# Pairing heads in a cached-decode attention kernel: one softmax chain, accumulator and eviction for two heads, and two value buffers instead of three

## The chip, the core and the metric

The kernel runs on one core of one Trainium2 chip. The core has five engines that follow instruction streams of their own: TensorE (PE, with its weight loads as PEld), VectorE (DVE), ScalarE (ACT), GpSimd (POOL) and SyncE (SP); SP issues nearly all loads here, and sixteen DMA engines carry them out. TensorE writes to PSUM, all else lies in SBUF. The metric is the device time of one execution in microseconds (us). The times of the kernel before are 528.05, 528.24 and 528.86 us, median 528.24.

## What is computed

One decode step for four sequences: a layer norm, attention over the last 2048 positions of a cache with 32 heads of width 192, and a gated feed-forward block beside it; the residual is added at the end. All inputs and the output are bf16.

```python
def _A_ref(x, k_cache, v_cache, wq, wo):
    B, Sq, D = x.shape                       # 4, 1, 640
    Hq, Dh = 32, 192
    Hkv, Sk = k_cache.shape[1], k_cache.shape[2]   # 32, 8192
    W = min(4096, max(256, Sk // 4))         # 2048
    q = (x @ wq).reshape(B, Sq, Hq, Dh).transpose(0, 2, 1, 3)
    k = k_cache[:, :, Sk - W:, :]
    v = v_cache[:, :, Sk - W:, :]
    scores = jnp.einsum("bhqd,bhkd->bhqk", q, k) * (Dh ** -0.5)
    p = _softmax(scores, axis=-1)
    o = jnp.einsum("bhqk,bhkd->bhqd", p, v)
    return o.transpose(0, 2, 1, 3).reshape(B, Sq, Hq * Dh) @ wo

def _B_ref(x, w1, w3, w2):                   # 640 -> 1536 -> 640
    return (silu(x @ w1) * (x @ w3)) @ w2

xn = _layernorm(x, axis=-1)
out = x + _A_ref(xn, A_k_cache, A_v_cache, A_wq, A_wo) + _B_ref(xn, B_w1, B_w3, B_w2)
```

## The kernel before

**Layout.** For each head, keys and values of all four sequences are one tile of 128 partitions: a partition holds 64 consecutive positions of one sequence (NJ = 64), 192 numbers each, 24 KB. So a key or value load is 3,072 KB, and there are 32 of each. wq (7.5 MB) is loaded at the start into the three value buffers, wo in eight loads of 960 KB, one for four heads; w1, w3 and w2 use key buffers at the end.

**Scores on VectorE.** Each query is broadcast to 128 partitions once per two heads (`q_bcast`, L207). A head is worked in four chunks of 16 positions (CH = 16, NC = 4). `mult` (L216) multiplies keys and query elementwise into a bf16 product tile `pr` of 16 x 192. `adder` (L225) adds slices of the product on TensorE: six matmuls (192/32) with the identity accumulate 16 x 32 sums in PSUM. `reduce_tile` (L233) finishes the sum over 32 on VectorE and writes 16 scores.

**Softmax chain.** After the last chunk of a head: the row maximum (`chain_lmax`, L243), its transpose on TensorE (`chain_tr`, L248), the maximum per sequence (`chain_gmax`, L253), its way back to all partitions by a matmul and the bias of each sequence (`chain_bc`, L261), four exponentials on ScalarE, one for each sequence, into a zero-padded tile `z`, each with its row sum. `rowsum` (L274) turns the row sums into a reciprocal.

**Values on TensorE.** `pv` (L281) runs 32 matmuls per head with `z` as weights and the values as moving data, 8 in each slot, into one PSUM accumulator; ScalarE evicts it to `o_sb`. `fold` (L297) adds the partial rows, and scales them. `ge_tr` (L308) and `ge_proj` (L315) transpose four heads' outputs and multiply them by their part of wo, into an accumulator held in PSUM over the whole kernel.

**Order.** The calls are put into slots, one for each chunk (128 in all), and phases within a slot; the calls are then made slot by slot. L363 to L404 hold the table: a load of keys eight slots ahead of the head's first product, a load of values nine slots after it less eight, `pv` nine slots after the chunk's product. This is the order in which the program is written; a scheduler in the compiler then sorts each engine's instructions by when it expects their inputs, with earlier calls first. An edge fixes one more thing: the reduction of chunk s comes after the product of chunk s + RLAG (L240, RLAG = 2). SP issues loads in its order, and an issue waits until the buffer that it will fill is free; whatever is behind it on SP waits too.

**Buffers.** Three for keys, three for values, four for products, three for `z`, two for wo.

**The end.** From slot 124 on w1, the last values, w3, the last part of wo and w2 are queued behind each other; the feed-forward matmuls run between the last heads' steps, and the last 160 KB of w2 release the last eight matmuls, an addition and two stores.

Of the kernel before, what the change touches and what calls it, by code (L numbers as in the profile page):

```python
# [18 lines left out]
def kernel(  # L19
# [12 lines left out]
    DD: int = 32,  # L32
    CH: int = 16,
    HG: int = 4,
    QP: int = 2,
    KBUFS: int = 3,
    VBUFS: int = 3,
    PBUFS: int = 4,
    NZ: int = 3,
    L: int = 9,  # L40
    RLAG: int = 2,
    ALIGN: int = 128,
):

    nc = tc.nc
# [14 lines left out]
    RPP = (HG * Dh) // P  # L62
    QW = QP * Dh
    OW = HG * Dh
# [4 lines left out]
    assert (HG * Dh) % P == 0 and Dh % RPP == 0 and H % HG == 0 and HG % QP == 0  # L69
# [10 lines left out]
    wpool = ctx.enter_context(tc.tile_pool(name="wstream", bufs=2))  # L80
    ppool = ctx.enter_context(tc.tile_pool(name="pr", bufs=PBUFS))
    qpool = ctx.enter_context(tc.tile_pool(name="qbc", bufs=2))
# [15 lines left out]
    def load_k(h):  # L98
        kt = kpool.tile([P, NJ, Dh], BF16, tag="kt")
        nc.sync.dma_start(out=kt[:], in_=cache_rows(A_k_cache, h))  # L100
        kts[h] = kt

    def load_v(h):
        vt = vpool.tile([P, NJ, Dh], BF16, tag="vt")
        nc.sync.dma_start(out=vt[:], in_=cache_rows(A_v_cache, h))
        vts[h] = vt

    def wo_load(hg):
        wt = wpool.tile([P, RPP * D], BF16, tag="w")
        nc.sync.dma_start(out=wt[:], in_=A_wo[hg * OW:(hg + 1) * OW, :].rearrange("(p i) n -> p (i n)", i=RPP))  # L110
        wos[hg] = wt

    x_sb = const.tile([B, D], BF16, name="x_sb")
# [12 lines left out]
    for r0 in range(0, KC, RV):  # L126
        r1 = min(r0 + RV, KC)
        wt = vpool.tile([P, RV, H * Dh], BF16, tag="vt")
        nc.sync.dma_start(out=wt[:, 0:r1 - r0, :], in_=wq_rows[:, r0:r1, :])  # L129
        wqs.append(wt)  # L130
# [9 lines left out]
    nsc = const.tile([1, B], FP32, name="nsc")  # L140
    nc.vector.memset(nsc[:], -SCALE)

    zs = []
    for i in range(NZ):
        z = const.tile([P, NJ // 2, 32], BF16, name=f"z{i}")
        nc.gpsimd.memset(z[:], 0.0)
        zs.append(z)
    oTs = []
    for i in range(2):
        oT = const.tile([P, RPP, 32], BF16, name=f"oT{i}")  # L150
        nc.gpsimd.memset(oT[:], 0.0)
        oTs.append(oT)
    rowsel = const.tile([P, 2 * B], FP32, name="rowsel")
    nc.vector.tensor_reduce(out=rowsel[:], in_=idf[:].rearrange("p (g c) -> p c g", g=NG)[:, 0:2 * B, :], axis=AX.X, op=ALU.add)
# [9 lines left out]
    sq = ppool.tile([B, D], FP32, tag="pr")  # L164
    ssq = const.tile([B, 1], FP32, name="ssq")
    nc.scalar.activation(out=sq[:], in_=xc[:], func=ACTF.Square, accum_out=ssq[:])
# [6 lines left out]
    xn = const.tile([B, D], BF16, name="xn")  # L173
# [13 lines left out]
    mbias = const.tile([P, B], FP32, name="mbias")  # L187
    nc.vector.tensor_scalar(out=mbias[:], in0=selT[:], scalar1=-1.0, scalar2=-MASK, op0=ALU.add, op1=ALU.mult)
# [27 lines left out]
    def mult(s):  # L216
        h, c = s // NC, s % NC
        pr = ppool.tile([P, CH, Dh], BF16, tag="pr")
        mi = nc.vector.tensor_tensor(out=pr[:], in0=kts[h][:, c * CH:(c + 1) * CH, :],  # L219
                                     in1=qbcs[h // QP][:, h % QP, :].unsqueeze(1).to_broadcast([P, CH, Dh]),  # L220
                                     op=ALU.mult)
        prs[s] = pr
        mult_insts[s] = mi

# [8 lines left out]
    def reduce_tile(s):  # L233
        h, c = s // NC, s % NC
        if c == 0:
            sc = small.tile([P, NJ], FP32, tag="sc", bufs=3)
            scs[h] = sc
        ri = nc.vector.tensor_reduce(out=scs[h][:, c * CH:(c + 1) * CH], in_=pss.pop(s)[:], axis=AX.X, op=ALU.add)  # L238
# [4 lines left out]
    def chain_lmax(h):  # L243
        lmax = small.tile([P, 1], FP32, tag="lmax")
        nc.vector.tensor_reduce(out=lmax[:], in_=scs[h][:], axis=AX.X, op=ALU.max)  # L245
        chs[h] = [lmax]

    def chain_tr(h):  # L248
        mt = ps_t.tile([P, P + B], FP32, tag="t")
        nc.tensor.transpose(out=mt[0:1, 0:P], in_=chs[h][0][:], identity=idf[:])  # L250
        chs[h].append(mt)

    def chain_gmax(h):  # L253
        gmax = small.tile([1, B], FP32, tag="gmax")
        nc.vector.tensor_reduce(out=gmax[:], in_=chs[h][1][0:1, 0:P].rearrange("o (q b) -> o b q", b=B),
                                axis=AX.X, op=ALU.max)
        gmq = small.tile([1, NQ, B], FP32, tag="gmq", bufs=1)
        nc.vector.tensor_copy(out=gmq[:], in_=gmax[:].unsqueeze(1).to_broadcast([1, NQ, B]))  # L258
        chs[h].append(gmq)

    def chain_bc(h):  # L261
        lmax, mt, gmq = chs.pop(h)
        sc = scs.pop(h)
        nc.tensor.matmul(mt[:, P:P + B], lhsT=gmq[:].rearrange("o q b -> o (q b)"), rhs=nsc[:], start=True, stop=True)  # L264
        negm = small.tile([P, B], FP32, tag="negm")
        nc.vector.tensor_tensor(out=negm[:], in0=mt[:, P:P + B], in1=mbias[:], op=ALU.add)  # L266
        z = zs[h % NZ][:].rearrange("p j (s b) -> p j s b", b=B)
        rs = small.tile([P, B], FP32, tag="rs")
        for b in range(B):
            nc.scalar.activation(out=z[:, :, 0:2, b], in_=sc[:].rearrange("p (j s) -> p j s", s=2), func=ACTF.Exp,  # L270
                                 bias=negm[:, b:b + 1], scale=SCALE, accum_out=rs[:, b:b + 1])
        rss[h] = rs

    def rowsum(h):  # L274
        tb = ps_t.tile([B, 1], FP32, tag="t")
        nc.tensor.matmul(tb[:], lhsT=rss.pop(h)[:], rhs=ones_f[:], start=True, stop=True)  # L276
        rcp = small.tile([B, 1], FP32, tag="rcp")
        nc.vector.reciprocal(out=rcp[:], in_=tb[:])  # L278
        rcps[h] = rcp

    def pv(s):  # L281
        h, c = s // NC, s % NC
        if c == 0:
            o_ps = ps_o.tile([P, 2 * Dh], FP32, tag="o_ps")
            o_pss[h] = o_ps
        o_ps, z, vt = o_pss[h], zs[h % NZ], vts[h]
        for jj in range(c * CH // 2, (c + 1) * CH // 2):
            g = jj % NG
            nc.tensor.matmul(o_ps[32 * g:32 * g + 32, :], lhsT=z[:, jj, :], rhs=vt[:, 2 * jj:2 * jj + 2, :],  # L289
                             start=(jj < NG), stop=(jj >= NJ // 2 - NG))  # L290
        if c == NC - 1:
            o_sb = opool.tile([P, 2, Dh], FP32, tag="o_sb")
            nc.scalar.copy(out=o_sb[:].rearrange("r two d -> r (two d)"), in_=o_pss.pop(h)[:])  # L293
            o_sbs[h] = o_sb
            vts.pop(h)

    def fold(h):  # L297
        hg, hl = h // HG, h % HG
        fp = ps_t.tile([B, Dh], FP32, tag="t")
        o_sb = o_sbs.pop(h)  # L300
        for two in range(2):
            nc.tensor.matmul(fp[:], lhsT=rowsel[:, two * B:(two + 1) * B], rhs=o_sb[:, two, :], start=(two == 0), stop=(two == 1))  # L302
        if hl == 0:
            o_bf = opool.tile([B, HG, Dh], BF16, tag="o_bf")
            o_bfs[hg] = o_bf
        nc.vector.tensor_scalar_mul(out=o_bfs[hg][:, hl, :], in0=fp[:], scalar1=rcps.pop(h)[:, 0:1])  # L306

    def ge_tr(hg):  # L308
        gp = ps_t.tile([P, RPP, B], BF16, tag="t")
        of = o_bfs.pop(hg)[:].rearrange("r h d -> r (h d)")  # L310
        for i in range(RPP):
            nc.tensor.transpose(out=gp[:, i, :], in_=of[:, i:OW:RPP], identity=idb[0:B, 0:B])  # L312
        nc.vector.tensor_copy(out=oTs[hg % 2][:, :, 0:B], in_=gp[:])  # L313

    def ge_proj(hg, i):  # L315
        oT = oTs[hg % 2]
        wo_t = wos[hg]
        st = (hg == 0 and i == 0)
        sp = (hg == H // HG - 1 and i == RPP - 1)
        for t in range(2):  # L320
            nc.tensor.matmul(acc[32 * t:32 * t + 32, :], lhsT=oT[:, i, :], rhs=wo_t[:, i * D + t * DH:i * D + (t + 1) * DH],  # L321
                             start=st, stop=sp)
# [44 lines left out]
    for h in range(H):  # L367
        s0 = h * NC
        if h >= KBUFS:
            add(s0 - (KBUFS - 1) * NC, 0, load_k, h)  # L370
        add(s0 + L + NC * (1 - VBUFS), 0, load_v, h)
        for c in range(NC):
            s = s0 + c
            add(s, 1, mult, s)
            add(s + 1, 2, adder, s)
            add(s + 2, 4, reduce_tile, s)
            add(s + L, 3, pv, s)
        e = s0 + NC - 1
        add(e + 2, 5, chain_lmax, h)
        add(e + 3, 4, chain_tr, h)  # L380
        add(e + 4, 5, chain_gmax, h)
        add(e + 5, 4, chain_bc, h)
        add(e + 6, 6, rowsum, h)
        add(s0 + NC - 1 + L + 1, 6, fold, h)
    for qg in range(H // QP):
        add(max(qg * QP * NC - 3, -1), 6, q_bcast, qg)
    for hg in range(H // HG):
        a = (hg + 1) * HG * NC - 1 + L
        add(hg * HG * NC + (4 if hg < H // HG - 1 else 14), 0, wo_load, hg)
        add(a + 2, 6, ge_tr, hg)  # L390
        for i in range(RPP):
            add(a + 3, 6, ge_proj, hg, i)
    hT = const.tile([P, CF, 32 * NF], BF16, name="hT")

    end = H * NC
    add(end - 4, 0, ffn_load, 1)
    add(end - 3, 1, ffn_load, 3)
    for n in range(NF):
        for c0, c1 in ((0, CF),) if n < NF - 1 else ((0, CF - 1), (CF - 1, CF)):
            add(end, 0, w2_load, n, c0, c1)  # L400
# [56 lines left out]
```

## Time and profile before

| what | us | where from |
|---|---|---|
| median of the runs | 528.24 | times |
| the profiled execution's own time | 528.51 | times |
| its span, first to last instruction | 526.6 | page |
| TensorE busy, matmuls | 360.0 (68%) | page, part 1 |
| VectorE busy | 340.2 (65%) | page, part 1 |
| ScalarE busy | 76.4 (15%) | page, part 1 |
| mean granted TensorE clock | 0.853 | clock by core |
| bytes read | 222.96 MB, 423 GB/s over the span | page, part 3 |
| product of one chunk (L219) | 1.745 each, x128 | page, part 5 |
| reduction of one chunk (L238) | 0.679 each, x128 | page, part 5 |
| adder matmul (L229) | 0.470 each, x768, 241.0 busy | page, part 5 |

The profile is one execution. Its first part gives the busy time of each engine; the second cuts the span into forty slices; the third lists the DMA queues with the time their packets took as a share of sixteen engines' span; the fifth lists groups of like instructions: busy time, mean length of one, and the idle time in front of them with what ended it. A timeline row gives the start, the length, the engine, the line, what is written and read, and in brackets the idle time before it. Two instructions of VectorE can overlap by some 0.07 us in their records, so the step from one start to the next is a little shorter than the length.

### The profile page before, as it was taken

Reading aid. Unit: us, or ns where it says so; the run is one execution under the profiler, and the core shown is the slowest. Engines: PE = TensorE matmul, PEld = TensorE weight load, DVE = VectorE, ACT = ScalarE, POOL = GpSimd, SP = SyncE. Lnnn points to the kernel's source line nnn. Section 1 sums busy time; section 2 is a strip of 40 time slices with the busy share of each in tenths; the row PEclk is TensorE's granted clock in tenths of the full one; section 3 lists DMA queues with packets and bytes.
Section 4 is the critical chain, followed back from the end, with each engine's and each line's share of the span. In section 5 each row is a group of like instructions: output and inputs, shape, how many; then the busy total and the mean of one; then the engine's idle time right before and its main releaser. Section 6 shows DMA issues by size and latency. Waiting matters only on the chain.

```text
span 526.6 us, 5872 instructions
## 1 busy us (share of the span) xinstructions
PE 360.0 (68%) x2384; PEld 148.4 (28%) x2384; DVE 340.2 (65%) x475; ACT 76.4 (15%) x318; POOL 4.5 (1%) x14
## 2 busy tenths in 40 slices
PE   1356767886676778767567976767678766668755
PEld 1122222332222333232222322223233322223322
DVE  4069766677666557777556677666567775665802
ACT  2101211101111111101111011111111011111130
POOL 3000000000000000000000000000000000000000
PEclk9999988778788887887878787888887887888888
DMA  8999999999999999999999999999999999999995
GB/s 359 439 425 437 429 429 431 432 424 435 437 429 435 429 434 429 433 432 431 429 433 428 426 440 426 437 429 431 432 433 431 429 436 430 431 426 440 423 426 218
DMA packets 11730, 223.33 MB, mean 424 GB/s; under 512 B 1316, under 2 KB 1464, under 8 KB 2872
## 3 DMA queue, kind: packets, MB, share of 16 engines
q1 hardware_dynamic: 11688, 222.97, 98.7%
q8 instruction: 18, 0.29, 0.2%
q14 instruction: 8, 0.07, 0.0%
q10 hardware_dynamic: 16, 0.01, 0.0%
HBM read 222.96 MB, written 0.01 MB: 423 GB/s over the span
## 4 chain that ended last, share of the span: by engine, by line
DMA 66%; DVE 21%; PE 9%; ACT 2%; issue 2%; SPq 0%; DVEq 0%; ACTq 0%
DMA kt<-in_A_k_cache_dram 61%; DVE pr L219 15%; PE ps L229 6%; DMA w2t<-in_B_w_dram 5%; DVE sc L238 5%; PE o_ps L289 1%; ACT z L270 1%; PE acc L321 1%; ACT o_sb L293 0%; DVE lmax L245 0%; SPq L129 0%; PE gp L312 0%; PE tb L276 0%; DVE rcp L278 0%; SPq L335 0%
## 5 line engine op out<-in xcount | busy, mean ns | idle before, releaser
L229 PE MATMUL ps<-pr,idb 128*128 128x512 bf16 x768 | 241.0, 470 | 110.4 <-DVE sc L238 101.1
L219 DVE TENSOR_TENSOR pr<-kt,qbc 128x3072 bf16<-128x3072 bf16 x128 | 223.3, 1745 | 35.5 <-DMA kt<-in_A_k_cache_dram 35.4
L229 PEld LDWEIGHTS <-idb 128*128 128x128 bf16 x768 | 85.3, 115 | 240.0 <-issue 190.4
L238 DVE TENSOR_REDUCE sc<-ps 128x16 f32<-128x512 f32 x128 | 86.9, 679 | 0.9 <-PE ps L229 0.9
L293 ACT COPY o_sb<-o_ps 128x384 f32<-128x384 f32 x32 | 15.1, 472 | 306.5 <-PE o_ps L289 306.5
L289 PE MATMUL o_ps<-vt,z 128*32 128x384 bf16 x1024 | 55.3, 334 | 3.8 <-DMA vt<-in_A_v_cache_dram 3.8
L270 ACT ACTIVATE z<-sc,negm 128x64 bf16<-128x64 f32 x128 | 45.7, 423 | 76.7 <-DVE negm L266 76.7
L266 DVE TENSOR_TENSOR negm<-mt,mbias 128x4 f32<-128x4 f32 x32 | 5.2, 161 | 70.7 <-PE mt L264 70.7
L306 DVE TENSOR_SCALAR o_bf<-fp,rcp 4x192 bf16<-4x192 f32 x32 | 12.9, 405 | 56.8 <-PE fp L302 29.9
L302 PE MATMUL fp<-o_sb,rowsel 128*4 128x192 f32 x128 | 26.7, 332 | 13.2 <-ACT o_sb L293 13.2
L289 PEld LDWEIGHTS <-z 128*32 128x32 bf16 x1024 | 25.0, 97 | 29.4 <-issue 20.8
L270 ACT ACTIVATION_READ_ACCUMULATOR z<-sc,negm 128x1 f32 x128 | 23.9, 187 | 0.0
L302 PEld LDWEIGHTS fp<-o_sb,rowsel 128*4 128x4 f32 x128 | 8.7, 87 | 24.2 <-ACT o_sb L293 18.6
L276 PE MATMUL tb<-ones_f,rs 128*4 128x1 f32 x64 | 6.2, 166 | 13.4 <-ACT z L270 13.4
L264 PE MATMUL mt<-nsc,gmq 1*128 1x4 f32 x64 | 12.2, 258 | 1.2 <-DVE gmq L258 1.2
L264 PEld LDWEIGHTS mt<-nsc,gmq 1*128 1x128 f32 x64 | 9.4, 183 | 12.1 <-issue 10.3
L276 PEld LDWEIGHTS tb<-ones_f,rs 128*4 128x4 f32 x64 | 3.6, 86 | 24.5 <-ACT z L270 23.0
L278 DVE RECIPROCAL rcp<-tb 4x1 f32<-4x1 f32 x32 | 4.9, 153 | 8.5 <-PE tb L276 8.5
L201 PE MATMUL qp<-wt,xnT 128*32 128x384 bf16 x80 | 7.0, 523 | 4.9 <-DMA wt<-in_A_wq_dram 4.9
L250 PE MATMUL mt<-idf,lmax 128*1 128x128 f32 x32 | 9.9, 308 | 0.5 <-DVE lmax L245 0.4
L321 PE MATMUL acc<-wt,oT 128*32 128x320 bf16 x96 | 9.7, 301 | 0.3 <-DVE oT L313 0.2
L213 ACT CAST qbc<-bp 128x384 bf16<-128x384 f32 x16 | 7.6, 485 | 7.7 <-PE bp L210 7.7
(61 smaller groups left out, 80.1 us busy)
## 6 DMA issues: line engine op xcount, KB each, us to landing
kt<-in_A_k_cache_dram SPq DMA_DIRECT2D x32, 3072.0 KB, 36.8
vt<-in_A_v_cache_dram SPq DMA_DIRECT2D x32, 3072.0 KB, 40.1
wt<-in_A_wo_dram SPq DMA_DIRECT2D x8, 960.0 KB, 36.5
wt<-in_A_wq_dram SPq DMA_DIRECT2D x2, 3072.0 KB, 13.2
wt<-in_B_w_dram SPq DMA_DIRECT2D x2, 1920.0 KB, 32.5
wt<-in_A_wq_dram SPq DMA_DIRECT2D x1, 1536.0 KB
w2t<-in_B_w_dram SPq DMA_DIRECT2D x2, 640.0 KB, 26.9
w2t<-in_B_w_dram SPq DMA_DIRECT2D x1, 480.0 KB, 27.6
```

Source lines behind the costliest of these rows:

```text
L219: mi = nc.vector.tensor_tensor(out=pr[:], in0=kts[h][:, c * CH:(c + 1) * CH, :], in1=qbcs[h // QP][:, h % QP, :].unsqueeze(1).to_broadcast ...
L229: nc.tensor.matmul(ps[:], lhsT=idb[:], rhs=pr[:, :, kk * DD:(kk + 1) * DD], start=(kk == 0), stop=(kk == NK - 1))
L238: ri = nc.vector.tensor_reduce(out=scs[h][:, c * CH:(c + 1) * CH], in_=pss.pop(s)[:], axis=AX.X, op=ALU.add)
L250: nc.tensor.transpose(out=mt[0:1, 0:P], in_=chs[h][0][:], identity=idf[:])
L264: nc.tensor.matmul(mt[:, P:P + B], lhsT=gmq[:].rearrange("o q b -> o (q b)"), rhs=nsc[:], start=True, stop=True)
L270: nc.scalar.activation(out=z[:, :, 0:2, b], in_=sc[:].rearrange("p (j s) -> p j s", s=2), func=ACTF.Exp, bias=negm[:, b:b + 1], scale=SCAL ...
L276: nc.tensor.matmul(tb[:], lhsT=rss.pop(h)[:], rhs=ones_f[:], start=True, stop=True)
L289: nc.tensor.matmul(o_ps[32 * g:32 * g + 32, :], lhsT=z[:, jj, :], rhs=vt[:, 2 * jj:2 * jj + 2, :], start=(jj < NG), stop=(jj >= NJ // 2 - NG))
L293: nc.scalar.copy(out=o_sb[:].rearrange("r two d -> r (two d)"), in_=o_pss.pop(h)[:])
L302: nc.tensor.matmul(fp[:], lhsT=rowsel[:, two * B:(two + 1) * B], rhs=o_sb[:, two, :], start=(two == 0), stop=(two == 1))
L306: nc.vector.tensor_scalar_mul(out=o_bfs[hg][:, hl, :], in0=fp[:], scalar1=rcps.pop(h)[:, 0:1])
L321: nc.tensor.matmul(acc[32 * t:32 * t + 32, :], lhsT=oT[:, i, :], rhs=wo_t[:, i * D + t * DH:i * D + (t + 1) * DH], start=st, stop=sp)
```

## The change

Heads are taken in pairs. Within eight heads the order is 0, 4, 1, 5, 2, 6, 3, 7 (`head`), so that the two of a pair lie four apart, and wo comes in four loads of 1,920 KB, each with two halves, into a single buffer. A chunk is 32 positions (64 slots in all); its adder has twelve matmuls of slices 16 wide. Of the four chunks of a pair the second has no adder: VectorE sums its product tile directly (`reduce_direct`). One chain serves the pair: two row maxima in one instruction, one transpose, one set of global maxima, one bias tile of eight columns, then eight exponentials into two `z` tiles, whose columns differ, so that both heads accumulate into one PSUM tile. One eviction, one fold and one row-sum step follow per pair. `pv` runs all 32 matmuls of a head in one call. There are two value buffers, three product buffers, two pairs of `z`; the reduction of chunk s follows the product of chunk s + 1. The third part of wq goes into the wo buffer.

```diff
-    DD: int = 32,
-    CH: int = 16,
-    HG: int = 4,
+    DD: int = 16,
+    CH: int = 32,
+    HG: int = 8,
     QP: int = 2,
     KBUFS: int = 3,
-    VBUFS: int = 3,
-    PBUFS: int = 4,
-    NZ: int = 3,
-    L: int = 9,
-    RLAG: int = 2,
-    ALIGN: int = 128,
+    VBUFS: int = 2,
+    PBUFS: int = 3,
+    NZ: int = 2,
+    L: int = 6,
+    RLAG: int = 1,
+    ALIGN: int = 96,
...
-    wpool = ctx.enter_context(tc.tile_pool(name="wstream", bufs=2))
+    wpool = ctx.enter_context(tc.tile_pool(name="wstream", bufs=1))
...
+    def head(j):
+        return j // HG * HG + j % HG // HH + j % HH * NPR
...
     def wo_load(hg):
-        wt = wpool.tile([P, RPP * D], BF16, tag="w")
-        nc.sync.dma_start(out=wt[:], in_=A_wo[hg * OW:(hg + 1) * OW, :].rearrange("(p i) n -> p (i n)", i=RPP))
+        wt = wpool.tile([P, HH, RPP * D], BF16, tag="w")
+        nc.sync.dma_start(out=wt[:], in_=A_wo[hg * HG * Dh:(hg + 1) * HG * Dh, :].rearrange(
+            "(hh p i) n -> p hh (i n)", hh=HH, i=RPP))
...
+    def reduce_direct(s):
+        nc.vector.tensor_reduce(out=score_tile(s), in_=prs.pop(s)[:], axis=AX.X, op=ALU.add)
...
+    def chain_bc(u):
+        lmax, mt, gmq = chs.pop(u)
+        sc = scs.pop(u)
+        nc.tensor.matmul(mt[:, P:P + I], lhsT=gmq[:].rearrange("o q b -> o (q b)"),
+                         rhs=nsc[:].rearrange("o h b -> o (h b)"), start=True, stop=True)
+        negm = small.tile([P, I], FP32, tag="negm")
+        nc.vector.tensor_tensor(out=negm[:], in0=mt[:, P:P + I], in1=mbias[:].rearrange("p h b -> p (h b)"), op=ALU.add)
+        rs = small.tile([P, I], FP32, tag="rs")
+        for i in range(I):
+            hh = i // B
+            z = zs[u % NZ * HH + hh][:].rearrange("p j (s i) -> p j s i", i=I)
+            nc.scalar.activation(out=z[:, :, 0:2, i], in_=sc[:, hh, :].rearrange("p (j s) -> p j s", s=2), func=ACTF.Exp,
+                                 bias=negm[:, i:i + 1], scale=SCALE, accum_out=rs[:, i:i + 1])
+        rss[u] = rs
...
+    def pv(j):
+        u, hh = j // HH, j % HH
+        if hh == 0:
             o_ps = ps_o.tile([P, 2 * Dh], FP32, tag="o_ps")
-            o_pss[h] = o_ps
-        o_ps, z, vt = o_pss[h], zs[h % NZ], vts[h]
-        for jj in range(c * CH // 2, (c + 1) * CH // 2):
+            o_pss[u] = o_ps
+        o_ps, z, vt = o_pss[u], zs[u % NZ * HH + hh], vts.pop(j)
+        for jj in range(NJ // 2):
             g = jj % NG
             nc.tensor.matmul(o_ps[32 * g:32 * g + 32, :], lhsT=z[:, jj, :], rhs=vt[:, 2 * jj:2 * jj + 2, :],
-                             start=(jj < NG), stop=(jj >= NJ // 2 - NG))
-        if c == NC - 1:
+                             start=(hh == 0 and jj < NG), stop=(hh == HH - 1 and jj >= NJ // 2 - NG))
+        if hh == HH - 1:
             o_sb = opool.tile([P, 2, Dh], FP32, tag="o_sb")
-            nc.scalar.copy(out=o_sb[:].rearrange("r two d -> r (two d)"), in_=o_pss.pop(h)[:])
-            o_sbs[h] = o_sb
-            vts.pop(h)
+            nc.scalar.copy(out=o_sb[:].rearrange("r two d -> r (two d)"), in_=o_pss.pop(u)[:])
+            o_sbs[u] = o_sb
...
+    PS = HH * NC
+    for j in range(H):
+        if j >= KBUFS:
+            add(NC * j - 3, 0, load_k, j)
+        add(NC * j + 2, 8, load_v, j)
+        add(NC * j + L, 3, pv, j)
+    for s in range(NS):
+        add(s, 1, mult, s)
+        if s % PS == 1:
+            add(s, 7, reduce_direct, s)
+        else:
+            add(s, 2, adder, s)
+            add(s + 1, 4, reduce_tile, s)
+    for u in range(H // HH):
+        e = u * PS + PS - 1
+        add(e + 1, 5, chain_lmax, u)
+        add(e + 1, 6, chain_tr, u)
+        add(e + 2, 5, chain_gmax, u)
+        add(e + 2, 6, chain_bc, u)
+        v = NC * (HH * u + 1) + L
+        add(v, 2, rowsum, u)
+        add(v + 1, 6, fold, u)
...
+    end = NS
     for hg in range(H // HG):
+        last = hg == H // HG - 1
+        a = NC * HG * hg
+        add(a + NC * HG - 2 if not last else end, 10, wo_load, hg)
+        add(a + NC * (HG - 1) + L + 2, 6, ge_tr, hg)
+        add(a + NC * (HG - 1) + L + (3 if not last else 5), 6, ge_proj, hg)
...
+    add(end - 2, 9, ffn_load, 1)
+    add(end, 9, ffn_load, 3)
     for n in range(NF):
         for c0, c1 in ((0, CF),) if n < NF - 1 else ((0, CF - 1), (CF - 1, CF)):
-            add(end, 0, w2_load, n, c0, c1)
+            add(end + 1, 0, w2_load, n, c0, c1)
     add(end // 2, 0, x_load)
-    add(end + L - NC, 0, ffn_mm, 1)
-    add(end + L + 1, 7, ffn_mm, 3)
-    add(end + L + 3, 7, ffn_transpose)
+    add(end + 3, 0, ffn_mm, 1)
+    add(end + 7, 0, ffn_mm, 3)
+    add(end + 8, 0, ffn_transpose)
```

## The prediction

> **What bounds the kernel now.** First the row of DMA shares over the span, then the queues, then the last microseconds in windows.
>
> ```profile
> DMA  8999999999999999999999999999999999999995
> GB/s 359 439 425 437 429 429 431 432 424 435 437 429 435 429 434 429 433 432 431 429 433 428 426 440 426 437 429 431 432 433 431 429 436 430 431 426 440 423 426 218
> q1 hardware_dynamic: 11688, 222.97, 98.7%
> q8 instruction: 18, 0.29, 0.2%
> ...
> 518.00:519.00 1.00, 0.13 (x3) 0.00 (x0) 0.21 (x1) 0.58 (x1) 0.00 (x0) 1.00 0.82 332
> 519.00:520.00 1.00, 0.73 (x12) 0.57 (x14) 0.55 (x2) 0.00 (x0) 0.00 (x0) 1.00 0.64 264
> 521.00:522.00 1.00, 0.34 (x6) 0.22 (x5) 0.39 (x2) 0.00 (x0) 0.00 (x0) 1.00 0.31 118
> 522.00:523.00 1.00, 0.56 (x10) 0.29 (x6) 0.00 (x0) 0.00 (x0) 0.00 (x0) 1.00 0.10 40
> ```
>
> The sixteen DMA engines never pause between the first and the last load: SP's queue alone fills 98.7% of the span. The kernel is bound by 223 MB at some 431 GB/s, and the change moves the same bytes. One key or value load of 3,072 KB takes 7.27 us in this queue: w1, queued ahead of it, is seen landed by its reader at 504.59, the last value load at 511.86. The windows (the last two columns are DMA share and GB/s) show a second thing: the engines do not finish together but between 518 and 523, and the slowest sets the end.
>
> Next the waits and the loads' own queue: can an engine ever starve a queue this deep?
>
> ```profile
> DVE pr L219 <- DMA kt<-in_A_k_cache_dram: 35.4, 18, 19.1
> PE ps L229 <- DVE sc L238: 101.1, 51, 4.8
> kt<-in_A_k_cache_dram SPq DMA_DIRECT2D x32, 3072.0 KB, 36.8
> vt<-in_A_v_cache_dram SPq DMA_DIRECT2D x32, 3072.0 KB, 40.1
> ```
>
> A load is issued 37 to 40 us before it lands, so some five loads of 7.27 us stand in the queue. VectorE waits for keys, not the other way round. Lateness of an engine up to about 30 us costs nothing now. That margin is what the change spends.
>
> Last, how long a head's chain takes. TensorE's records matter here.
>
> ```profile
> 485.68 1.76 DVE L219 TENSOR_TENSOR pr<-kt,qbc 128x3072 bf16<-128x3072 bf16 x1
> 487.35 0.68 DVE L238 TENSOR_REDUCE sc<-ps 128x16 f32<-128x512 f32 x1
> 488.09 4.23 PE L229 MATMUL ps<-pr,idb 128*128 128x512 bf16 x12 [2.67 <-DVE sc L238]
> 492.75 1.46 PE L229 MATMUL ps<-pr,idb 128*128 128x512 bf16 x6 [0.32 <-DVE sc L238]
> 494.13 1.16 PE L289 MATMUL o_ps<-vt,z 128*32 128x384 bf16 x24
> 511.86 2.75 PE L289 MATMUL o_ps<-vt,z 128*32 128x384 bf16 x32 [3.81 <-DMA vt<-in_A_v_cache_dram]
> ```
>
> After an idle of two microseconds or more a matmul of 512 columns takes 0.43 us (5.28 for twelve elsewhere), in a stream 0.23 (1.46 for six). A product of 3072 elements steps in 1.67 us, a 512-element reduction in 0.60. The order on an engine is not the order of the schedule: the 24 value matmuls belong to slots before the adder that runs ahead of them, so work whose input comes late is sorted behind what is ready sooner.
>
> **The change, part by part.** All in trace time against this execution's span, 526.6 us; its own time was 528.51, and the median of the runs shown is 528.24, so I add 1.6 to a span to get a time.
>
> *Saved work that is hidden.* One of four chunks loses its adder: 192 of 768 matmuls of 0.31 (241.0/768), 60 us of TensorE. Chain, eviction and fold run per pair, 16 times for 32: evictions alone 16 x 0.47 = 7.6 us of ScalarE; exponentials stay 128. All of it runs under the loads: nothing on the path.
>
> *Longer VectorE pieces.* A product of 32 positions is 2 x 1.67, about 3.3. The direct reduction takes 6144 bf16 elements from SBUF; no row shows it. From the nearest reductions (64 elements 0.21, 512 elements 0.68, so 1.05 ns each) it is 6.6; from the product's rate of two bf16 elements a cycle, 3.3. I take 6.5: every reduction here goes at one element per cycle. The Trainium skill (VectorE: DVE Perf Modes, "The perf-mode tier table") says that tensor_reduce has only the single-rate program, bf16 in SBUF too; by it 6144 elements at 0.96 GHz are an estimate of 6.4. Per pair VectorE then has 4 x 3.3 + 3 x 0.6 + 6.5 + 1.4 (row maximum, two global steps, bias, reciprocal, fold) = 23 of the 29.1 us that four loads take (7 us spare): busier, not the bound. The adder's rows become runs of 16 elements instead of 32; no row shows a price: 0 to a doubling (2.8 us per chunk while warm, two chunks of it in the first chain); I take 0, as the two states above differ by the clock alone.
>
> *Two value buffers for three.* Value load j now waits for the value matmuls of head j-2. In steady state, with an even head's keys landing at 0: products to 3.3 and 7.2, row maximum and reductions to 9 (adder cold), global maximum 9.5, direct reduction to 16, bias 16.2, four exponentials (0.35 apart) 17.7, value matmuls cold 2.75 to 20.4, and the next value load's data start some 1.2 later (x's tiny load, issued at 0.73, is read at 2.19, 1.46 in all), 21.6. The queue ahead (three loads after the key landing) is busy until 4 x 7.27 = 29.1. Spare: 7 us. It stays fed, about two loads deep instead of five.
>
> *The last pair.* Behind the last keys (landing at 14.5 on that scale) there are no further keys, so only one value load stands before V(30): busy until 21.8 against 21.6. I take 0; with the value matmuls sorted behind the adder (below) 5.5.
>
> *The first pair.* Here it does not fit. Keys land at 30.3, 37.6, 44.9, the queue goes on V(0) 52.1, K(3) 59.4, V(1) 66.7, K(4) 73.9, and V(2) must then be there. V(2) reuses V(0)'s buffer, so it needs pair 0's softmax: products 30.3 to 36.9; the cold adder 33.7 to 38.9 and its reduction 39.5; direct reduction 46.0; products 49.3, 52.6; adder cold to 54.4, reduction 55.0; the product of the next pair, which the issue-order edge puts before the last reduction, 58.3; that reduction 58.9; another ready product 62.2; row maximum, a reduction, global maximum 63.5; the next pair's direct reduction, ready while the bias makes its trip through TensorE, 70.0; bias 70.2; table load 1.28 and four exponentials 1.4 to 72.9; value matmuls cold to 75.6; data 76.8. That is 2.9 late. If the direct reduction is sorted ahead of the first small one, 1.0 late. If the chain goes ahead of both the other product and the second direct reduction (-9.8), in time by 6.9. I take 1.8. Queued behind V(2) on SP is K(5), which is then late by as much and no more.
>
> *Instruction fetch.* Completion events in the trace show, per load, all sixteen engines within 0.6 us at first; the last one falls to 2.1 behind right after the first 16 KB packet of queue q8 (27.5), to 3.4 after the ninth (258), to 4.8 after the seventeenth (484). Packets go round eight engines, and each costs its engine some 1.5 us. TensorE's 2384 matmuls and as many weight loads are 4768 instructions in 18 packets, 265 to a packet. The change has 192 + 16 + 32 + 32 + 64 + 24 = 360 fewer pairs, 4048 instructions: 15 packets (4048/265), so no engine is hit three times: -1.4, and 0 at the other end. The Trainium skill (Runtime: NRT & Kernel Launch, "Instruction fetch mechanics") gives 256 instructions to a block, which the 18 packets agree with; that the crossing is mostly hidden, as it also says, does not hold for the slowest engine here, and by it the -1.4 would be 0. But a gap at V(2) lets all engines start level again, and the others still take two hits after it; so the two don't add: the end moves by the larger of -1.4 and the lateness.
>
> *Wo in loads of 1,920 KB, one buffer.* The previous projection ends seven slots before the next load is issued, and SP has four issues of 0.58 fewer: 0. At the end the last projection reads 1,920 KB instead of 960 just before w2; 24 matmuls take 2 us (0.99 for twelve) after a landing 4.5 before w2's: 0, and 1.3 if TensorE is cold.
>
> Sum: 526.6 + 1.8 = 528.4, time 530.0.
>
> **The rivals.**
> *Nowhere dry, one fetch hit less* (not slower). It needs V(2) in time. For it: with the chain put first V(2) is there at 76.8 - 9.8 = 67.0. Against: VectorE takes whatever is ready while a chain makes its trip. Decides at 73.9. Then 526.6 - 1.4, time 526.8.
> *Value matmuls behind the adder.* If adder and value matmuls come ready together (exponentials end at 17.7, the odd product at 19.5), the adder's 5.1 us go first and the value matmuls follow warm (1.5): 19.5 + 5.1 + 1.5 + 1.2 = 27.3 at the last pair, 5.5 late, and at the start 73.5 + 5.1 + 1.5 + 1.2 = 81.3, 7.4 late; either or both: time 535 to 541. For it: the schedule lists the adder first in each slot. Against: late work is sorted back above.
> *Starved in every pair.* If besides that the direct reduction delays the odd head's product by more than the 1.8 us that would then be left (29.1 - 27.3), each of 15 pairs loses 1 to 2: time 543 to 558. Against: VectorE's 23 of 29.1.
> *The direct reduction at two elements a cycle.* Twice 3.3 less before V(2): 70.2, in time; the time is that of the first rival.
>
> **How the numbers follow.** Forecast (dry once, 1 to 3 late) 0.44; nowhere dry, by either rival, 0.23; behind the adder 0.19; starved 0.08; small lateness with most of the -1.4 lost, 0.06. 0.2% is 1.06 us, about what a measurement of this kernel can tell. Faster: 0.22 of nowhere dry. Same: its other 0.01, 0.13 of the forecast (its low end), 0.05 of the last. Slower: 0.31 + 0.19 + 0.08 + 0.01 = 0.59. The range 526.4 to 538 leaves out starving and the worst of the third case; the forecast's own is 529.2 to 531.2.
>
> **What would show it.** The DMA row dips once, near 74; V(2)'s issue at about 75.6; q8 has 15 packets; issue to landing 13 to 22 us; direct reductions of 6.5. Wrong if the dip is absent, or if it comes back in every pair.

## The result, and the profile after

The changed kernel takes 533.83 us (median of six runs, 532.67 to 534.55) against 528.35 for the kernel before in the same set (528.05 to 531.32): ratio 1.0092, 95% interval 1.0068 to 1.0117. It is slower, and by 3.8 us more than the forecast of 530.0. The profiled execution took 534.16 us with a span of 532.4, 5.8 more than the span before.

The page of the changed kernel: the DMA rows over the span, the queues, and the two loads' time from issue to landing.

```profile
DMA  8999989999999999999999999999999999998995
GB/s 359 439 424 432 439 332 437 425 432 438 425 431 438 430 430 430 437 430 430 426 439 432 428 432 438 426 430 438 415 441 432 430 436 431 430 433 362 412 420 206
q1 hardware_dynamic: 11624, 222.97, 97.8%
q8 instruction: 16, 0.26, 0.2%
...
kt<-in_A_k_cache_dram SPq DMA_DIRECT2D x32, 3072.0 KB, 28.2
vt<-in_A_v_cache_dram SPq DMA_DIRECT2D x32, 3072.0 KB, 22.0
```

The bytes are the same and the middle of the row is as full as before. But the row dips twice, in the slices at 66.5 to 80 us (332 GB/s) and at 479 to 492 (362). A value load is now issued 22.0 us before it lands, not 40.1: three loads of 7.27 stand in the queue, five and a half did before.

The waits of VectorE and TensorE, and the SP queue's own (total, times, longest):

```profile
PE ps L243 <- DVE pr L226: 88.8, 18, 10.1
...
DVE pr L226 <- DMA kt<-in_A_k_cache_dram: 70.8, 13, 18.0
```

```profile
SPq L113 <- PE o_ps L304: 252.3, 26, 20.7
```

VectorE still waits for keys, for 70.8 us in all, so it is not the bound. What is new is on SP: 26 of the value loads wait for the value matmuls (L304) to give a buffer back, up to 20.7 us each. In the kernel before 7 of them did, 3.2 us at most:

```profile
SPq L105 <- PE o_ps L289: 21.8, 7, 3.2
```

The first dip in the timeline: VectorE's work on the first two heads, then the value matmuls and the issue of the third value load, V(2) (counted from 0).

```profile
36.76 6.55 DVE L254 TENSOR_REDUCE sc<-pr 128x32 f32<-128x6144 bf16 x1
...
43.22 0.68 DVE L248 TENSOR_REDUCE sc<-ps 128x32 f32<-128x512 f32 x1
...
58.69 0.28 DVE L258 TENSOR_REDUCE lmax<-sc 128x2 f32<-128x128 f32 x1
58.88 6.54 DVE L254 TENSOR_REDUCE sc<-pr 128x32 f32<-128x6144 bf16 x1
...
65.34 0.27 DVE L268 TENSOR_REDUCE gmax<-mt 2x4 f32<-2x128 f32 x1
...
69.75 2.75 PE L304 MATMUL o_ps<-vt,z 128*32 128x384 bf16 x32 [3.24 <-issue]
...
72.54 0.54 SPq L113 DMA_DIRECT2D vt<-in_A_v_cache_dram  x1
```

Two direct reductions of 6.5 us stand in the first chain: pair 0's own, and pair 1's, which VectorE takes while pair 0's maximum makes its trip through TensorE. V(2) is issued at 72.54. The stretches around it (the last two columns are DMA share and GB/s; a packet counts in the stretch in which it starts, so a short one can rise over 1):

```profile
71.00:72.00 1.00, 1.00 (x20) 0.58 (x13) 1.00 (x1) 0.00 (x0) 0.00 (x0) 0.50 0.12 49
...
72.50:73.00 0.50, 0.50 (x2) 0.20 (x3) 0.50 (x1) 0.00 (x0) 0.00 (x0) 0.50 0.00 0
73.00:73.50 0.50, 0.50 (x3) 0.15 (x1) 0.24 (x1) 0.00 (x0) 0.00 (x0) 0.50 0.00 0
73.50:74.00 0.50, 0.50 (x2) 0.15 (x1) 0.00 (x0) 0.00 (x0) 0.00 (x0) 0.50 1.16 295
```

The queue runs empty before V(2)'s first data move. By the completion events in the trace (in the timeline's time, as all landings below) the load ahead, K(4), lands on its last engine at 73.49 and V(2) at 82.57: 9.08 us, where 7.27 is the step of a full queue. The end is 1.8 us late from here on.

The second dip, in the timeline of the last pair:

```profile
469.90 3.36 DVE L226 TENSOR_TENSOR pr<-kt,qbc 128x6144 bf16<-128x6144 bf16 x1 [3.71 <-DMA kt<-in_A_k_cache_dram]
...
477.23 6.54 DVE L254 TENSOR_REDUCE sc<-pr 128x32 f32<-128x6144 bf16 x1
...
485.70 0.17 DVE L280 TENSOR_TENSOR negm<-mt,mbias 128x8 f32<-128x8 f32 x1 [0.69 <-PE mt L277]
...
487.58 2.75 PE L304 MATMUL o_ps<-vt,z 128*32 128x384 bf16 x32 [1.91 <-ACT z L285]
...
490.28 1.96 PE L243 MATMUL ps<-pr,idb 128*128 128x512 bf16 x6
```

```profile
488.00:490.00 2.00, 2.00 (x32) 0.96 (x25) 2.00 (x2) 0.86 (x6) 0.00 (x0) 0.50 0.54 233
490.00:492.00 2.00, 2.00 (x14) 0.86 (x8) 2.00 (x1) 0.00 (x0) 0.00 (x0) 0.67 0.56 160
```

The value matmuls run ahead of the adder here, 20.4 us after the keys came (469.90 to 490.33). V(30), issued right behind them, lands 8.64 us after the load ahead of it: 1.4 late.

The last load lands at 527.28, against 523.28 before. What follows it up to the end of the span, the tail, is longer too: 5.1 us against 3.3. In this execution TensorE ran at half clock there (the column before the DMA share):

```profile
524.00:526.00 2.00, 2.00 (x18) 1.13 (x16) 0.00 (x0) 0.00 (x0) 0.00 (x0) 0.50 0.85 331
526.00:528.00 2.00, 2.00 (x20) 1.12 (x16) 0.80 (x2) 0.00 (x0) 0.00 (x0) 0.50 0.03 11
```

So the span's 5.8 us are 4.0 up to the last landing and 1.8 behind it. Of the 4.0, the pauses make 1.8 + 1.4; about 0.8 is left, and it fits the instruction fetch. In the trace before, the sixteen completions of a load lie 0.6 us apart at first, and 2.1, 3.4 and 4.8 after packets 1, 9 and 17 of q8. The trace does not name the engines, but packets 2 to 8 make other completions late and leave the last one where it is; packet 9 delays a late one again. In the trace after, a pause lets all engines start level again (0.65 apart after the first, 0.5 after the second), but level with the slowest. Then packets 2 (to 1.9) and 10 (to 3.0), and after the second pause packet 15 (to 1.8), move the last completion. The chain of slowest engines has four hits in it, 1, 2, 10 and 15, where it had three.

### The profile page after: what moved, and what is told of

The parts are those of the page before. It is cut to its first block, busy times and chain, and to the rows that moved or that the text cites. A ratio compares the mean times of both kernels' runs of the same rounds, so it can differ in the third digit from the quotient of the medians.

```text
span 532.4 us, 4873 instructions
## 1 busy us (share of the span) xinstructions
PE 296.2 (56%) x2024; PEld 127.9 (24%) x2024; DVE 371.7 (70%) x247; ACT 70.2 (13%) x302; POOL 5.3 (1%) x14
## 4 chain that ended last, share of the span: by engine, by line
DMA 49%; DVE 26%; PE 19%; issue 3%; ACT 1%; SPq 1%; ACTq 0%; DVEq 0%
DMA kt<-in_A_k_cache_dram 46%; DVE pr L226 13%; DVE sc L254 10%; PE ps L243 8%; PE o_ps L304 6%; DMA vt<-in_A_v_cache_dram 3%; PE acc L334 2%; DVE sc L248 2%; ACT z L285 1%; PE mt L277 1%; SPq L113 1%; PE ff L440 1%; DVE o_bf L320 1%; PE gt L357 0%; PE gp L326 0%
## 5 line engine op out<-in xcount | busy, mean ns | idle before, releaser
L226 DVE TENSOR_TENSOR pr<-kt,qbc 128x6144 bf16<-128x6144 bf16 x64 | 212.9, 3350 | 74.6 <-DMA kt<-in_A_k_cache_dram 70.8
L243 PE MATMUL ps<-pr,idb 128*128 128x512 bf16 x576 | 172.9, 469 | 88.9 <-DVE pr L226 88.8
L243 PEld LDWEIGHTS <-idb 128*128 128x128 bf16 x576 | 64.9, 115 | 186.0 <-issue 137.1
L254 DVE TENSOR_REDUCE sc<-pr 128x32 f32<-128x6144 bf16 x16 | 104.7, 6543 | 0.0
L304 PE MATMUL o_ps<-vt,z 128*32 128x384 bf16 x1024 | 67.9, 426 | 32.3 <-ACT z L285 23.0
L248 DVE TENSOR_REDUCE sc<-ps 128x32 f32<-128x512 f32 x48 | 32.8, 685 | 25.6 <-PE ps L243 25.6
L277 PE MATMUL mt<-nsc,gmq 2*128 2x8 f32 x32 | 9.2, 358 | 69.5 <-DVE gmq L271 69.5
L304 PEld LDWEIGHTS <-z 128*32 128x32 bf16 x1024 | 30.3, 118 | 62.1 <-issue 29.8
L285 ACT ACTIVATION_READ_ACCUMULATOR z<-sc,negm 128x1 f32 x128 | 40.7, 318 | 0.0
L277 PEld LDWEIGHTS mt<-nsc,gmq 2*128 2x128 f32 x32 | 7.8, 301 | 76.6 <-DVE gmq L271 76.3
L316 PE MATMUL fp<-o_sb,rowsel 128*8 128x192 f32 x64 | 14.1, 347 | 1.0 <-ACT o_sb L308 1.0
```

What stands on the lines that cost most here:

```text
L226: mi = nc.vector.tensor_tensor(out=pr[:], in0=kts[j][:, c * CH:(c + 1) * CH, :], in1=qbcs[h // QP][:, h % QP, :].unsqueeze(1).to_broadcast ...
L243: nc.tensor.matmul(ps[:], lhsT=idb[:], rhs=pr[:, :, kk * DD:(kk + 1) * DD], start=(kk == 0), stop=(kk == NK - 1))
L248: ri = nc.vector.tensor_reduce(out=score_tile(s), in_=pss.pop(s)[:], axis=AX.X, op=ALU.add)
L254: nc.vector.tensor_reduce(out=score_tile(s), in_=prs.pop(s)[:], axis=AX.X, op=ALU.add)
L277: nc.tensor.matmul(mt[:, P:P + I], lhsT=gmq[:].rearrange("o q b -> o (q b)"), rhs=nsc[:].rearrange("o h b -> o (h b)"), start=True, stop=True)
L285: nc.scalar.activation(out=z[:, :, 0:2, i], in_=sc[:, hh, :].rearrange("p (j s) -> p j s", s=2), func=ACTF.Exp, bias=negm[:, i:i + 1], sca ...
```

## The experiments

They were timed in three sets, each beside the kernel before. It took 529.15 us beside the versions without a direct reduction at the two ends, with adders everywhere, with two key buffers, and the kernel before with two value buffers in its first form; 529.58 beside each end alone, the 45 matmuls and the larger fetch; 528.91 beside the rest.

**No direct reduction at the two ends.** The rows point at the direct reduction in pairs 0, 1 and 15. They get the adder back; the other thirteen pairs keep the direct reduction.

```diff
-        if s % PS == 1:
+        if s % PS == 1 and 1 < s // PS < NS // PS - 1:
```

> The changed kernel with the adder in place of the direct reduction in the first two pairs and the last one only; the other thirteen pairs keep it. Theory: only these three matter, so the time is that of the variant without any direct reduction within 1 us (528 to 530.5), and no spot is dry in between. Rival (each pair loses a little to the direct reduction): halfway or less of the loss is won back, 531.5 or more.

It took 527.12 us, ratio 0.9960 (0.9944 to 0.9975): faster than both kernels, and than was expected. From its page and its timeline:

```profile
DMA  8999999999999999999999999999999999999996
...
q1 hardware_dynamic: 11624, 222.97, 99.0%
q8 instruction: 16, 0.26, 0.2%
```

```profile
61.07 2.75 PE L304 MATMUL o_ps<-vt,z 128*32 128x384 bf16 x32 [3.52 <-issue]
63.87 0.53 SPq L113 DMA_DIRECT2D vt<-in_A_v_cache_dram  x1
```

Both dips are gone: V(2) is issued 8.7 us sooner. With two value buffers and direct reductions in the middle the queue stays fed, and the last load lands at 521.90. That is 1.4 us sooner than before, what one hit by a fetch packet costs; with 16 packets no engine takes a third.

**Each end alone.** First the adder in pairs 0 and 1 only, then in pair 15 only.

```diff
-        if s % PS == 1:
+        if s % PS == 1 and s // PS > 1:
```

> The changed kernel with the adder in place of the direct reduction in the first two pairs only. Theory: the dry spot near 74 us goes, the one near 490 stays. The engines then keep their different lateness instead of starting level, so the slowest has two fetch hits before 490 instead of one before and two after the first spot: the last load lands 1.8 (dry) + 2.4 (two hits after it) - 1.5 (one hit kept) = 2.7 us earlier than 527.5, time 531.1 (530.3 to 532). Rival (dry spots add, fetch hits don't matter): 1.8 earlier, time 532.0; rival (a late start is caught up later): no change, 533.8.

```diff
-        if s % PS == 1:
+        if s % PS == 1 and s // PS < NS // PS - 1:
```

> The changed kernel with the adder in place of the direct reduction in the last pair only. Theory: the dry spot near 74 stays (1.8 for the slowest engine), the one near 490 goes (1.4), and with it the hit that follows it (1.2): the last load lands 2.6 us earlier than 527.5, time 531.2 (530.4 to 532). Rival (V(30) is waited for by nothing that counts): 533.8.

They took 530.18 (ratio 1.0015, 1.0003 to 1.0028) and 530.13 (1.0016, 1.0002 to 1.0030), each a little less than was expected. The DMA row of the first, then of the second:

```profile
DMA  8999999999999999999999999999999999998996
```

```profile
DMA  8999989999999999999999999999999999999996
```

Each keeps exactly the dip of the other end. The last landing moves from 527.28 to 524.44 (-2.8) and 524.55 (-2.7), close to the -2.7 and -2.6 that were expected; both together give -5.4. The pauses add up, and each is worth its lateness (1.8, 1.4) and about one fetch hit more (1.0, 1.3).

**Adders everywhere.**

```diff
-        if s % PS == 1:
+        if False:
```

> The changed kernel without the direct reduction: all four chunks of a pair go through the adder. Theory: the two direct reductions of 6.5 us that stand before the first pair's value matmuls, and the one before the last, are gone; the third value load is issued some 8 us earlier (about 64 instead of 72.5), V(30) some 6 us earlier, neither spot is dry; TensorE's code grows by 384 instructions to 17 packets. Time 528 to 530.5. Rival (pairing and two buffers do it, whoever sums): 532.5 or more, dry spots kept.

528.69 us, ratio 0.9987 (0.9973 to 1.0000); no dip in the row, 17 packets of q8, last landing 523.46. Beside the kernel with direct reductions in the middle, in the same set, it is 1.6 us slower, so VectorE's thirteen long reductions cost nothing there. The 156 matmuls that they save are one packet, but that packet is not the whole difference. With adders everywhere the last value load, V(31), is issued at 496.57 instead of 495.11; the DMA share falls to 0.68 from 497 to 498 (1.14 in the other kernel), and V(31) lands 0.9 later (508.95 against 508.01). The other 0.6 comes behind it, with packet 17 at 512.98. Why V(31) is issued later was not tested.

**Three value buffers after the change, two key buffers.** A key buffer is given up for it, so that the count stays at five; key loads and w2's loads move to where their buffers come free.

```diff
-    KBUFS: int = 3,
-    VBUFS: int = 2,
+    KBUFS: int = 2,
+    VBUFS: int = 3,
...
-            add(NC * j - 3, 0, load_k, j)
+            add(NC * j - 2, 0, load_k, j)
...
-            add(end + 1, 0, w2_load, n, c0, c1)
+            add(end + 4, 0, w2_load, n, c0, c1)
```

> The changed kernel with three value and two key buffers: the count of five is kept, the value buffer that the first and the last pair wait for is given back (key loads are issued one slot later, w2 three slots later, as the buffers demand). Theory: no dry spot near 74 and 490 us, DMA share 0.97 or more there, the sixteen engines land up to 3 us apart to the end, and the last load lands 4 to 5.5 us earlier than at 527.5: time 528 to 530. Rival: five buffers are too few in either split, or another part of the change costs the time: 532 or more.

530.7 us, ratio 1.0030 (1.0014 to 1.0045), just above what was expected; the last landing, 525.26, is 2.0 earlier and not 4 to 5.5. The two dips are gone (DMA share 0.91 from 72 to 76, full from 488 to 492), but there is another at the start, since the third key load waits for head 0's products:

```profile
35.00:40.00 5.00, 3.76 (x9) 1.18 (x8) 4.96 (x2) 0.00 (x0) 0.00 (x0) 1.00 0.48 162
```

So the dips do come from the value buffers, and the direct reduction can stay where a third one covers it; the pause only moves to whichever buffer is scarce.

**Two value buffers in the kernel before.** Is the second buffer alone the cost?

```diff
-    VBUFS: int = 3,
+    VBUFS: int = 2,
```

> The kernel before with two value buffers and nothing else changed. Theory: what makes two buffers too few is the long way from a key landing to the value matmuls of a pair, not the count itself. Here the first head's value matmuls end at about 59 us, and the third value load is wanted at 73.9: the queue stays fed, also at the end, and the time is that of the kernel before within 0.5 us (ratio 0.999 to 1.001). Rival: two value buffers alone make the queue run dry at the same places, +3 us or more (ratio 1.006 and up).

539.12 us, ratio 1.0170 (1.0145 to 1.0195), which was not foreseen. The row shows no dip, and the last load lands at 523.5 (523.3 before). But its last load is another one. A value load's slot is worked out from the number of buffers; with two, V(31) falls four slots later, behind w2. The last head's whole work then stands behind the last landing (timeline, then windows):

```profile
523.53 2.75 PE L289 MATMUL o_ps<-vt,z 128*32 128x384 bf16 x32 [14.43 <-DMA vt<-in_A_v_cache_dram]
```

```profile
524.00:538.60 14.60, 10.04 (x97) 4.51 (x85) 2.46 (x7) 1.06 (x2) 0.00 (x0) 0.70 0.00 0
```

The kernel tells nothing of the buffers' price, only of the order. With w3, the last part of wo and w2 put behind V(31) it does:

```diff
-    VBUFS: int = 3,
+    VBUFS: int = 2,
...
-        add(hg * HG * NC + (4 if hg < H // HG - 1 else 14), 0, wo_load, hg)
+        add(hg * HG * NC + (4 if hg < H // HG - 1 else 17), 2 if hg == H // HG - 1 else 0, wo_load, hg)
...
-    add(end - 3, 1, ffn_load, 3)
+    add(end + 1, 1, ffn_load, 3)
...
-            add(end, 0, w2_load, n, c0, c1)
+            add(end + 1, 3, w2_load, n, c0, c1)
```

> The kernel before with two value buffers, and with w3, the last part of wo and w2 queued behind the last value load, as they are with three buffers. In the first run with two value buffers the queue was fed to the end (last landing 523.5, 523.4 in the kernel before); the 10 us went into the work behind the last landing, because the formula for the slot of a value load put V(31) behind w2. Theory: with the order of the end mended, two value buffers cost this kernel nothing: last landing 523.4, 3.3 us behind it, time that of the kernel before within 0.6 us. Rival (two buffers cost at the ends also here): 1.5 us or more.

528.92 us, ratio 0.9991 (0.9973 to 1.0009), last landing 523.1. With a chain for each head and no direct reduction, two value buffers cost nothing. The lateness needs both: the scarce buffer, and 6.5 or 13 us of direct reduction ahead of its release.

**More instructions to fetch.** The kernel before with slices of 8 instead of 32: four times the adder matmuls, each a quarter as wide, and 36 packets of q8 instead of 18.

```diff
-    DD: int = 32,
+    DD: int = 8,
```

> The kernel before with adder slices 8 wide instead of 32: four times as many adder matmuls of a quarter of the columns, 4608 more instructions for TensorE, so some 36 packets on the fetch queue instead of 18; loads, buffers and the order are kept. Theory: packets go round eight engines and cost each 1.2 to 1.5 us, so the engine hit first is hit five times instead of three: engines land 7 to 8 us apart at the end (4.8 before), the last load 2.4 to 3 us later, time 531 to 531.5. Rival (fetching is hidden behind the loads): 528.4, engines 5 us apart or less.

532.63 us, ratio 1.0064 (1.0044 to 1.0085), 3.05 above the kernel before. The last loads of this kernel in windows:

```profile
519.00:521.00 2.00, 1.50 (x15) 0.53 (x15) 0.58 (x2) 0.00 (x0) 0.00 (x0) 0.50 0.61 255
...
525.00:527.00 2.00, 2.00 (x18) 1.16 (x16) 0.68 (x2) 0.00 (x0) 0.00 (x0) 0.50 0.09 36
```

Some engines are done by 519, the last at 526.28, 7.6 us apart; it was 4.8. The end of the loads moves by 3.0, which is two extra hits of up to 1.5 on the slowest engine. Fetch packets of 16 KB, 0.4% of the DMA time, set the end of this kernel.

**The tail.** Is the half clock behind the last landing a cost of the change? Unused matmuls on w1 are put ahead of the tail, 45 of them, then 105, to keep TensorE busy; their sums are thrown away.

```diff
+    def warm():
+        gt = ps_t.tile([P, NCH], FP32, tag="t")
+        for kc in range(KC):
+            for n in range(NF):
+                nc.tensor.matmul(gt[32 * n:32 * n + 32, :], lhsT=xnT[:, kc, :],
+                                 rhs=ffn[1][:, kc, n * NCH:(n + 1) * NCH],
+                                 start=(kc == 0), stop=(kc == KC - 1))
...
+    for _ in range(3):
+        add(end + 3, 1, warm)
```

> The changed kernel with 45 more matmuls (w1 against the input, three times over, results unused) behind the first feed-forward matmuls at about 508 us, where TensorE idles six microseconds. Theory: TensorE then runs at full clock from the last value matmuls on, the work behind the last landing (4.9 us in the changed kernel, 3.3 in the kernel before) shrinks by 0.7 to 1.7 us, the landings stay where they are: time 532.1 to 533.1. Rival (the larger last wo load makes the end longer, not the clock): 533.8.

533.54 us, ratio 1.0080 (1.0062 to 1.0098). It decided nothing: the added matmuls were over at 510, the clock was at half again by 515, and the tail was 4.4 us. With `range(7)`, beside the changed kernel once more as it is:

> The changed kernel with 105 more matmuls at 506 us instead of the 45 of the run before, so that TensorE has no idle between w1's landing and the last values' (513.6); results unused. The 45 ended at 510.2 and the full clock was lost again by 515. Theory: the clock is full from 513.6 to the end, the work behind the last landing takes 3.3 to 3.8 us instead of 4.9, the landings stay: time 532.2 to 532.8. Rival (not the clock): 4.4 or more behind the last landing.

> The changed kernel once more, on the same chip as the others of this set, to be compared with them: 533.8 (532.7 to 534.6), dry spots near 74 and 490, last landing near 527.5.

With 105 matmuls the granted clock is 1.00 from 510 on and the tail 3.4 us, yet the time is 533.23 (1.0069, 1.0047 to 1.0092), more than was expected and the same as the unchanged one's 533.13 (1.0075, 1.0050 to 1.0100). The profile of that unchanged kernel says why:

```profile
524.00:526.00 2.00, 2.00 (x19) 1.35 (x16) 0.27 (x1) 0.00 (x0) 0.00 (x0) 0.50 0.72 283
526.00:528.00 2.00, 1.84 (x22) 1.23 (x18) 0.66 (x3) 0.00 (x0) 0.00 (x0) 0.85 0.06 21
```

The same program has the full clock back for most of its last two busy microseconds here, and a tail of 3.5 us; its last load lands at 527.36, where the other execution's was at 527.28. So the 1.8 us of longer tail were seen in one execution of the changed kernel and not in the other, and the two medians of this set show no cost in them. What sets the clock there is not shown.

**Both together.** The kernel with direct reductions in the middle only, plus the 105 matmuls.

```diff
-        if s % PS == 1:
+        if s % PS == 1 and 1 < s // PS < NS // PS - 1:
...
+    for _ in range(7):
+        add(end + 3, 1, warm)
```

> The changed kernel with the adder in the first two pairs and the last one, and with the 105 unused matmuls at about 506 us. Theory: no dry spot, 16 or 17 packets and so the slowest engine hit twice (last landing 522.0 as in the run without the matmuls, or 523.3 if the added code makes a seventeenth packet count), and a full clock at the end: 3.3 us behind the last landing instead of 3.5. Time 526.6 to 528.4; 0.1 to 0.4% below the kernel before. Rival: no better than without the matmuls, 527.1 or more.

528.54 us, ratio 0.9981 (0.9966 to 0.9996), just above what was expected. In the profiled execution q8 has 17 packets again and the last load lands at 523.2, 1.3 later than without the matmuls; packet 17, at 520.93, makes the last completion 1.5 late. The code that warms the engine costs the fetch hit that was saved. The version without it stays the best of all.

## Why the prediction was right, and where it fell short

The direction, the bound and the first of the two places were right; the sum was 1.8 us and the span shows 5.8. The time lies outside the 529.2 to 531.2 that the forecast gave for its own case, and inside the whole range only because that covered other cases too; so much is luck. Of the signs, the dip near 74 came, but it was to be the only one, and there is a second at 490.

*Saved work, hidden: 0.* Right. TensorE's matmuls went from 360.0 to 296.2 us busy and ScalarE from 76.4 to 70.2, and nothing of it was seen in the time.

*Direct reduction: 6.5.* Right, from the part of the page by groups:

```profile
L226 DVE TENSOR_TENSOR pr<-kt,qbc 128x6144 bf16<-128x6144 bf16 x64 | 212.9, 3350 | 74.6 <-DMA kt<-in_A_k_cache_dram 70.8
L243 PE MATMUL ps<-pr,idb 128*128 128x512 bf16 x576 | 172.9, 469 | 88.9 <-DVE pr L226 88.8
...
L254 DVE TENSOR_REDUCE sc<-pr 128x32 f32<-128x6144 bf16 x16 | 104.7, 6543 | 0.0
```

It took 6.54 us, twice the product of as many elements (3.35); the rival with two elements a cycle is out. The Trainium skill (VectorE: DVE Perf Modes, "The perf-mode tier table") has a single rate alone for this reduction; the row agrees. Runs of 16 elements cost the adder nothing: 469 ns a matmul, 470 before, at a mean granted clock that was lower (0.753 against 0.853).

*Steady state, fed.* Right. Between the two dips the row holds nines, and issue to landing is at the end of the 13 to 22 us that were given.

*First pair: 1.8 late.* The size, 1.8 as well, is right by luck, by errors that cancel. V(2) was issued at 72.54, not at 75.6: the direct reduction ran ahead of the first small one (36.76), the order for which 1.0 was given, and the issue came 1.2 sooner than that order's 73.7. But the restart cost 1.6 more, and K(4) landed 0.4 sooner (73.49, not 73.9): 1.0 - 1.2 + 1.6 + 0.4 = 1.8.

*Restart: 1.2.* This is the term that was mis-sized. A load issued into an empty queue lands 10.0 to 10.1 us after its issue (V(2), V(30); wq's first load, at the start of the trace, 9.9), 2.8 more than the 7.27 that it adds to a full queue. The records of single packets around V(2) show what was left out: 24 KB take 0.91 us on an engine in a full queue, but here the first start 1.4 to 2.4 us after the issue and most take 1.1 to 1.7. And the working compared the start of data with a landing; K(4)'s last packet ended at 73.17 and was landed at 73.49, so the queue wanted new data 0.3 us before the landing.

*Last pair: "I take 0".* This step failed by it. The chain was right to the tenth: value matmuls at 20.4 after the keys. With 2.8 in place of 1.2 the data are at 23.2 on that scale against 21.8; 1.4 late, and 1.4 were measured. A margin of 0.2 us on a term known from one tiny load should have counted as late.

*Fetch: "the end moves by the larger of -1.4 and the lateness".* Wrong. There were 16 packets, not 15 (4048/265 is 15.3, so a sixteenth is begun), and the kernel without dips shows the -1.4. But with a pause in between it is not merely lost: levelling puts every engine at the slowest one's time, and hits of different engines, which ran side by side, come one after the other, four for three. The lateness comes with about 0.8 on top, somewhat less than one more hit; that it is this hit is worked out from the spread of the completions, and the runs with each end alone agree with it. The Trainium skill (Runtime: NRT & Kernel Launch, "Instruction fetch mechanics") calls the crossing to a new block mostly hidden; for TensorE that may stand, for the loads it does not, by 36 packets (+3.0) and by 16 (-1.4).

*Tail: 0, or 1.3 with TensorE cold.* The cold case came in one profile (1.8) and not in another (0.2).

Together 1.8 + 1.4 + 0.8 + 1.8 = 5.8 for the profiled execution. The rivals: nowhere dry was not what happened, but its working holds for the kernel that has it (526.8 worked out, 527.12 measured). The value matmuls were not sorted behind the adder (487.58 against 490.28), though the time comes close to that rival's: its lateness of 5.5 at the last pair alone would make 533.7, which its 535 to 541 leave out. And no pair between the ends starved.

## What to carry to other kernels

Where every transfer shares one full queue, as here, look for the price of a change that thins it at its two ends, where fewer loads stand ahead of the late one; work out the issue time there, and leave the cheap but slow form of the work to the middle. Count a pause at its restart price, and count a margin smaller than the uncertainty of that price as spent. A depth that is also used in a schedule's formulas moves loads past each other, so look at the order of the queue after every change of it.

## What the runs showed of the hardware

- A restart of an empty load queue costs 2.8 us from issue to landing over the 7.27 of a 3,072 KB load in a full one.
- A pause levels the sixteen DMA engines (from 1.8 and 3.05 us apart to 0.65 and 0.5), so delays that lay on different engines add across pauses.
- One 16 KB packet of instructions delays one engine's loads by 1.2 to 1.5 us; in the trace before, packets 1, 9 and 17 are those that move the last completion. 36, 18 and 16 packets in kernels without a dip in the row put the last landing at 526.28, 523.28 and 521.90.
- The same program ended one execution at half clock and another at nearly full clock, with tails of 5.1 and 3.5 us.
